# Weights of two modes and strided rows of two batches, each in one transfer

## The chip, the core and the metric

One NeuronCore of a Trainium2 chip runs the whole program. The metric is device time in microseconds (us), of which a run gives one value. A profile is one execution, taken by the hardware profiler; its span (first to last instruction) is mostly some 1.8 us shorter than the device time of the same run (438.82 us of time and 436.9 of span). PE is the matmul engine, DVE the vector engine, ACT the scalar engine, POOL is GpSimd, which here does little but issue transfers (315 of its 339 instructions in the profile of before).

## The reference

Attention of 8 batches, 8 heads, 576 positions, 64 columns per head: heads 0 to 3 see a window of 32 positions ("local"), heads 4 to 7 every 32nd position ("strided"). Its output `x` (8 x 576 x 512) goes through a spectral mix:

```
X = rfft(x, axis=1)[:, :64]                 # 64 modes
Yr = X.real @ w_r[m] - X.imag @ w_i[m]      # per mode m, w_r and w_i: 64 x 512 x 512
Yi = X.real @ w_i[m] + X.imag @ w_r[m]
u = x + irfft(Y)
out = u + relu(u @ w_ch)
```

w_r and w_i are 134 of the 163 MB that the kernel reads. They are float32 in HBM; the transfers turn them into float16 on their way to SBUF (163.22 MB read from HBM in the profile of before, 81.29 MB in the packets of GpSimd's queue, which brings all but the constants).

## The kernel before

GpSimd issues all loads of rows and weights. The modes are passed twice, first for the half of the columns that the strided heads make, then for the other half; numbers from 0 to 127 count the modes of both passes, so that 64 + 51 is mode 51 of the second pass. Each mode has a tile of 4 KB per partition, w_r in partitions 0 to 63, w_i in 64 to 127, and two transfers of 256 KB:

```python
GUEST = {3: ("Y0", 0), 4: ("Y0", 1), 5: ("X0", 0), 6: ("X0", 1)}
GUEST |= {15: ("YT", 0), 16: ("YT", 1)}     # six modes live in tiles that are needed later
...
def w_fetch(n=1):
    for _ in range(n):
        ...
        wt = pw.tile([128, 4, DM], F16, tag="w", name="wt")      # NWBUF = 11 buffers
        for ri, src in enumerate([moe_w_r, moe_w_i] if m else [moe_w_r]):
            nc.gpsimd.dma_start(
                wt[ds(64 * ri, 64)],
                src[m, ds(256 * half, 256), :].rearrange("(p c) e -> p c e", c=4),
            )
```

A mode is 16 matmuls (4 x 4, each 128x128 by 16 columns), after which the next tile is fetched. In the second pass other work lies between the modes: pieces that transpose the attention's output and multiply it by w_ch, about 1.1 per mode, and two per mode in the last ten (`LATE`) before the output stage:

```python
LATE = 10
first = len(work) - 2 * LATE
for m in range(NM - 3):
    mode(1, m)
    if m < NM - 3 - LATE:
        upto = -(-first * (m + 1) // (NM - 3 - LATE))
    else:
        upto = first + 2 * (m - (NM - 4 - LATE))
    for w in work[n:upto]:
        w()
    ...
    if m >= 16 and m % 16 in (4, 8):
        spec(m // 16 - 1, 0 if m % 16 == 4 else 1)
```

Then comes the output stage: 36 blocks of rows, each an inverse transform on PE, a relu on ACT (`rl`), an add on DVE (`osb`), and the store. w_ch, rl and osb took their buffers from the weights' pool.

The softmax here doesn't subtract the row's maximum and nothing guards it: scores larger than these inputs give would overflow.

Of the kernel before, what the change touches and what calls it, by code (L numbers as in the profile page):

```python
# [10 lines left out]
FP = mybir.dt.float32  # L11
F16 = mybir.dt.float16
# [6 lines left out]
DM = 512  # L19
NM = 64  # L20
# [3 lines left out]
JG = [(0, 6), (6, 11), (11, 16)]  # L24
SCALE = float(1.0 / np.sqrt(D))
NEG = -30000.0
NWBUF = 11


def _host_consts():  # L30
# [49 lines left out]
def kernel(  # L80
# [10 lines left out]
    nc = tc.nc  # L91
# [3 lines left out]
    big = ctx.enter_context(tc.tile_pool(name="big", bufs=1))  # L95
# [5 lines left out]
    def psum_pools(**bufs):  # L101
        pctx.close()
        for n, c in bufs.items():
            pss[n] = pctx.enter_context(
                tc.tile_pool(name="ps_" + n, bufs=c, space=PSUM)
            )

    def psum(kind, half=False):
        if half:
            return pss[kind].tile([128, 1024], F16, tag=kind, name=kind)  # L110
        return pss[kind].tile([128, 512], FP, tag=kind, name=kind)
# [16 lines left out]
    def const_load(eng, *which):  # L128
        for n in which:
            eng.dma_start(cs[n][:, 0 : hosts[names.index(n)].shape[1]], drams[n])  # L130
# [13 lines left out]
    def spectra_tile(n):  # L144
        if n == "X0":
            Xh[0] = big.tile([128, 4, B, 2, NM], F16, tag=n, name=n)
        else:
            YS[n] = big.tile([128, 4, 4, 16, 16], F16, tag=n, name=n)

    xb = [px.tile([128, 11, 256], F16, tag="xb", name="xb") for _ in range(B)]  # L150

    pw = ctx.enter_context(tc.tile_pool(name="pw", bufs=NWBUF))
    actx = ctx.enter_context(ExitStack())
# [3 lines left out]
    ring = pat.tile([128, 12, 2048], F16, name="ring")  # L157
# [8 lines left out]



    GUEST = {3: ("Y0", 0), 4: ("Y0", 1), 5: ("X0", 0), 6: ("X0", 1)}
    GUEST |= {15: ("YT", 0), 16: ("YT", 1)}  # L170
    guests = {}
    w_tiles = []
    w_chs = {}

    def w_fetch(n=1):
        for _ in range(n):
            i = len(w_tiles)
            if i >= 2 * NM:
                return
            half, m = 1 - i // NM, i % NM  # L180
            if i in GUEST:
                n, j = GUEST[i]
                if j == 0:
                    guests[n] = big.tile([128, 2, 4, DM], F16, tag=n, name="wt")
                wt = guests[n][:, j]
            else:
                wt = pw.tile([128, 4, DM], F16, tag="w", name="wt")

            for ri, src in enumerate([moe_w_r, moe_w_i] if m else [moe_w_r]):
                nc.gpsimd.dma_start(  # L190
                    wt[ds(64 * ri, 64)],
                    src[m, ds(256 * half, 256), :].rearrange("(p c) e -> p c e", c=4),
                )
            w_tiles.append(wt)

    def w_ch_fetch():
        w_ch = pw.tile([128, 4, DM], F16, tag="w", name="w_ch")
        nc.gpsimd.dma_start(w_ch, moe_w_ch.rearrange("(c p) e -> p c e", p=128))
        w_chs["n"] = w_ch

# [3 lines left out]
    SRC = {2: v, 0: q, 1: k}  # L204
    SLOT = {2: 0, 0: 1, 1: 2}

    def str_in(b, vi):
        return ring[0:72, 3 * (b % 4) + SLOT[vi], :]
# [2 lines left out]
        t = ring[:, ds(2 * (b % 6), 2), :].rearrange("p n x -> p (n x)")  # L211
        return t[:, ds(1152 * vi, 1152)]

    def load_str(b):
        for vi in (2, 0, 1):
            nc.gpsimd.dma_start(
                str_in(b, vi)[0:64],
                SRC[vi][b, 4:8].rearrange("h (c r) d -> (h c) (r d)", r=32)[0:64],
            )
            if b % 2 == 0:  # L220
                n = 3 * (b % 4) + SLOT[vi]
                nc.gpsimd.dma_start(
                    ring[64:72, n : n + 4 : 3, :],
                    SRC[vi][b : b + 2, 4:8].rearrange(
                        "b h (c r) d -> (h c) b (r d)", r=32
                    )[64:72],
                )

    def load_loc(*bs):
        for b in bs:  # L230
            if b >= B:
                return
            for vi in (2, 0, 1):
                nc.gpsimd.dma_start(
                    loc_in(b, vi),
                    SRC[vi][b, 0:4].rearrange("h (cb i) d -> (h cb) (i d)", i=18),
                )
# [294 lines left out]
    def mode(slot, m):  # L532
        half = 1 - slot
        mi, mg = m % 8, m // 8
        if mi == 0:
            ypt[slot] = psum("y")
        yp = ypt[slot]
        yv = yp.rearrange("p (m e x) -> p m e x", m=8, e=4)
        wt = w_tiles[slot * NM + m]
        pr = ds(0, 128 if m else 64)  # L540
        for e in range(4):
            for c in range(4):
                nc.tensor.matmul(  # L543
                    yv[:, mi, e, :],
                    wt[pr, XC[c], ds(128 * e, 128)],
                    Xh[half][pr, c, :, :, m],
                    start=(c == 0),
                    stop=(c == 3),
                )
        if slot or m not in GUEST:  # L550
            w_fetch()
        ends = {7: 8}
        if slot and mg == 7:
            ends = {5: 6, 7: 2}
        if mi in ends:
            n = ends[mi]
            m0 = mi + 1 - n
            part = (
                slice(None),
                slice(None),  # L560
                mg // 2,
                slice(None),
                ds(8 * (mg % 2) + m0, n),
            )
            src = yp.rearrange("p (m e x) -> p e x m", m=8, e=4)[:, :, :, ds(m0, n)]
            if slot == 0:
                if m == 7:
                    spectra_tile("Y0")
                nc.scalar.activation(out=YS["Y0"][part], in_=src, func=ACTF.Copy)
            else:  # L570
                nc.vector.tensor_tensor(
                    out=YS["YT"][part], in0=src, in1=YS["Y0"][part], op=AluOp.add
                )
# [117 lines left out]


    psum_pools(tp=3, sc=3, av=2)
    load_str(0)
    const_load(nc.scalar, "cI", "cM6", "cM5", "cFs")
    load_str(1)
    const_load(nc.sync, "cMl", "cFl", "cA")
    load_str(2)
    w_fetch(2)

    def str_front(b):
        return [
            lambda: str_v(b, 0), lambda: str_v(b, 1),
            lambda: str_v(b, 2), lambda: str_q(b, 0),
            lambda: str_back(b, 0),
            lambda: str_back(b, 1), lambda: str_q(b, 1),
            lambda: str_k(b, 0),
            lambda: str_k(b, 1), lambda: str_k(b, 2),
        ]

    def loc_front(b):
        if b >= B:
            return [lambda: None] * 8
        return [
            lambda: loc_turn(b, 0, 0), lambda: loc_turn(b, 0, 1),
            lambda: loc_turn(b, 1, 0), lambda: loc_turn(b, 1, 1),
            lambda: loc_turn(b, 2, 0), lambda: loc_turn(b, 2, 1),
            lambda: loc_back(b, 0), lambda: loc_back(b, 1),
        ]
# [19 lines left out]
                )  # L739
    SPLIT = [0, 2, 4, 5, 7, 8, 10]  # L740
    for b in range(B):
        if b < 5:
            load_str(b + 3)
        load_loc(*[(), (), (), (), (0,), (1, 2), (3,), (4, 5)][b])
        w_fetch([3, 3, 2, 2, 2, 1, 1, 1][b])
        front = str_front(b + 1) if b + 1 < B else loc_front(0)
        for t in range(6):
            str_scores(b, t)
            if b > 0:
                if t < 2:  # L750
                    str_values(b - 1, 4 + t)
                elif t == 2:
                    dft(b - 1, 1)
            if t >= 2:
                str_values(b, t - 2)
            for w in front[SPLIT[t] : SPLIT[t + 1]]:
                w()
        if b == 1:
            nc.vector.memset(PL[:, 0:PS0], 0.0)
# [10 lines left out]
    for b in range(B):  # L770
# [12 lines left out]
        n = 0  # L783
        nm = NMODES[b]
        for mi in range(nm):
# [3 lines left out]
            n = upto  # L789
# [5 lines left out]
    ptr = ctx.enter_context(tc.tile_pool(name="ptr", bufs=1))  # L795
# [37 lines left out]
    n = 0  # L833
# [3 lines left out]
    for m in range(NM - 3):  # L837
# [7 lines left out]
        n = upto  # L845
# [11 lines left out]
    held, vps, ups, rls, osbs = {}, {}, {}, {}, {}  # L857
# [5 lines left out]
    def pool_adds(b, t):  # L863
        if (b, t) in ((0, 1), (B - 1, 3)):
            return False
        return t in (1, 3, 4) or (b, t) in ((2, 2), (4, 2))
# [21 lines left out]
    def v_rows(i):  # L888
        b, t = units[i]
        if i not in vps:  # L890
            v_early(i)
        vp = vps.pop(i)
        rows_of(b, t, vp, zzs, False)
        if t % 2 == 0:
            rls[b, t] = rls[b, t + 1] = pw.tile([128, 2, DM], FP, tag="w", name="rl")
        rl = rls[b, t][:, t % 2, :]
        nc.scalar.activation(out=rl, in_=vp, func=ACTF.Relu)  # L897
        if pool_adds(b, t):
            nc.gpsimd.tensor_tensor(out=rl, in0=rl, in1=x_rows(b, t), op=AluOp.add)  # L899
# [48 lines left out]
    for m in range(NM - 3, NM):  # L948
        mode(1, m)
# [6 lines left out]
    for i in range(len(units)):  # L956
        v_rows(i)
        b, t = units[i]
# [42 lines left out]
```

## Time and profile before

| | before |
|---|---|
| device time, median of 3 runs | 437.79 us (437.7 to 438.99) |
| span of the profiled run | 436.9 us |
| DMA engines at 90% or more | about 6 to 393 us |
| GpSimd transfers (weights, all) | 254, 315 |
| PE waiting for weights, 120 to 366 us | 59.3 us |
| PE waiting for weights, after 366 us | 0.8 us |
| modes 62, 63 of the second pass start | 397.04, 397.51 us |

### The profile page before, as it was taken

To read this page: it belongs to the slowest core of one execution; us is meant where nothing else is said; L and a number is where in the kernel's file an instruction comes from. 1 tells how busy PE (TensorE), PEld (TensorE's weight loads), DVE (VectorE), ACT (ScalarE), POOL (GpSimd) and SP (SyncE) were. 2 spreads that over 40 slices of the span, in tenths; PEclk is the share of its full clock that TensorE was granted. 3 is DMA by queue.
4 is the path that set the end of the run, shared out by engine and by line. 5 is a ranking of instruction groups with operands and counts; after the bars stand their busy time and mean duration, and the time that the engine had idled before them with its cause. 6 is when DMAs were issued, how large, how long until landed. Compare 5 with 4: busy or idle time off the path is not lost.

```text
span 436.9 us, 12328 instructions
## 1 busy us (share of the span) xinstructions
PE 334.7 (77%) x5289; PEld 240.8 (55%) x5289; DVE 216.1 (49%) x466; ACT 188.5 (43%) x353; POOL 186.6 (43%) x339
## 2 busy tenths in 40 slices
PE   1977888789887888978884576777585948988994
PEld 1866776657756665766653344454354535654441
DVE  2887778835425233344311133344335443773895
ACT  1686678635544345435442211124022402442882
POOL 6545453333343344434343443443443444320883
PEclk9998899959968768688755558689778868998998
DMA  8999999999999999999999999999999999991687
GB/s 173 206 213 211 211 212 211 210 211 211 213 210 212 213 207 211 212 212 212 212 210 212 212 212 212 211 213 211 198 213 212 211 212 212 211 202 25 265 324 278
DMA packets 31094, 92.20 MB, mean 211 GB/s; under 512 B 6144, under 2 KB 7168, under 8 KB 31040
## 3 DMA queue, kind: packets, MB, share of 16 engines
q0 software_dynamic: 26800, 81.29, 94.5%
q1 hardware_dynamic: 3440, 9.46, 5.8%
q10 hardware_dynamic: 800, 0.67, 0.6%
q8 instruction: 42, 0.69, 0.6%
q14 instruction: 12, 0.10, 0.1%
HBM read 163.22 MB, written 9.44 MB: 395 GB/s over the span
## 4 chain that ended last, share of the span: by engine, by line
DMA 55%; PE 26%; DVE 10%; issue 4%; ACT 2%; POOL 1%; DVEq 0%; POOLq 0%
DMA wt<-in_moe_w_i_dram 49%; DMA wt<-in_moe_w_r_dram 5%; PE y L543 3%; PE sc L641 3%; DVE kz L288 2%; DVE xb L246 2%; PE u L684 2%; PE v L684 2%; PE sc L510 2%; PE v L886 2%; DMA ring<-in_q_dram 2%; PE tp L320 1%; PE sc L349 1%; PE av L370 1%; PE sc L341 1%
## 5 line engine op out<-in xcount | busy, mean ns | idle before, releaser
L543 PE MATMUL y<-X,wt 128*128 128x16 f16 (+1 forms) x2048 | 82.7, 193 | 62.6 <-DMA wt<-in_moe_w_i_dram 60.1
L190 POOL DMA_DIRECT2D wt<-in_moe_w_r_dram x128 | 65.8, 514 | 117.4 <-DMA wt<-in_moe_w_r_dram 25.9
L543 PEld LDWEIGHTS <-wt 128*128 128x128 f16 (+1 forms) x2048 | 72.2, 103 | 77.1 <-issue 55.4
L190 POOL DMA_DIRECT2D wt<-in_moe_w_i_dram x126 | 64.8, 514 | 69.7 <-DMA wt<-in_moe_w_i_dram 51.7
L650 ACT ACTIVATE v<-sc 128x512 f16<-128x512 f32 x32 | 19.0, 597 | 88.3 <-PE sc L641 88.3
L641 PE MATMUL sc<-w_cp,xT 128*128 128x512 f16 (+1 forms) x160 | 48.2, 428 | 0.5 <-DVE xT L613 0.4
L467 ACT ACTIVATE PL<-sc 128x480 f16<-128x480 f32 (+1 forms) x48 | 27.6, 579 | 45.0 <-PE sc L453 44.7
L651 DVE COPY xo<-tp 128x512 f16<-128x512 f16 x32 | 22.1, 692 | 39.7 <-PE tp L649 39.7
L246 DVE TENSOR_TENSOR xb<-av,rec 90x256 f16<-90x256 f32 (+2 forms) x80 | 36.0, 450 | 2.8
L245 DVE RECIPROCAL rec<-av 90x4 f32<-90x4 f32 (+2 forms) x80 | 14.7, 184 | 43.2 <-PE av L482 32.1
L398 DVE COPY qT<-tp 128x576 f16<-128x576 f16 x16 | 12.0, 758 | 38.5 <-PE tp L391 35.0
L256 ACT ACTIVATE v<-tp 128x640 f16<-128x640 f16 (+1 forms) x24 | 19.4, 808 | 20.4 <-PE tp L425 17.1
L356 ACT ACTIVATE PL<-sc 90x360 f16<-90x360 f32 (+1 forms) x48 | 22.9, 489 | 9.5 <-PE sc L349 8.8
L391 PE MATMUL tp<-cI_s,ring 64*64 64x64 f16 x864 | 25.4, 208 | 1.9 <-DVE kz L398 1.2
L899 POOL TENSOR_TENSOR rl<-rl,xo 128x512 f32<-128x512 f32 x16 | 18.3, 1156 | 19.2 <-ACT rl L897 18.8
L916 DVE TENSOR_TENSOR osb<-u,rl 128x512 f32<-128x512 f32 x36 | 23.6, 688 | 2.6 <-PE u L684 1.3
L391 PEld LDWEIGHTS <-ring 64*64 64x64 f16 x864 | 20.1, 121 | 6.7 <-issue 3.7
L437 PE MATMUL sc<-cMl_s,cI_s 128*128 128x480 f16 (+1 forms) x48 | 22.5, 469 | 1.6 <-ACT X L256 1.6
L281 PE MATMUL tp<-cI_s,ring 72*128 72x72 f16 x256 | 15.0, 207 | 10.7 <-DMA ring<-in_v_dram 8.0
L453 PE MATMUL sc<-qT,kz 128*128 128x160 f16 (+1 forms) x160 | 22.6, 269 | 0.3 <-issue 0.3
L593 DVE COPY xT<-tp 128x512 f16<-128x512 f16 x16 | 11.0, 689 | 22.9 <-PE tp L587 22.8
L897 ACT ACTIVATE rl<-v 128x512 f32<-128x512 f32 x36 | 20.4, 597 | 4.2 <-PE v L684 3.5
(98 smaller groups left out, 648.4 us busy)
## 6 DMA issues: line engine op xcount, KB each, us to landing
wt<-in_moe_w_r_dram POOLq DMA_DIRECT2D x128, 256.0 KB, 9.4
wt<-in_moe_w_i_dram POOLq DMA_DIRECT2D x126, 256.0 KB, 9.6
out_dram<-osb SPq DMA_DIRECT2D x14, 512.0 KB, 2.7
ring<-in_v_dram POOLq DMA_DIRECT2D x8, 288.0 KB, 10.4
ring<-in_q_dram POOLq DMA_DIRECT2D x8, 288.0 KB, 10.6
ring<-in_k_dram POOLq DMA_DIRECT2D x8, 288.0 KB, 10.6
ring<-in_v_dram POOLq DMA_DIRECT2D x8, 256.0 KB, 8.4
ring<-in_q_dram POOLq DMA_DIRECT2D x8, 256.0 KB, 8.4
```

The source lines that it names most:

```text
L190: nc.gpsimd.dma_start(wt[ds(64 * ri, 64)], src[m, ds(256 * half, 256), :].rearrange("(p c) e -> p c e", c=4),)
L246: nc.vector.tensor_tensor(out=dst, in0=val.rearrange("p h (q c) -> p h c q", c=4), in1=rec[0:n, 0:pieces] .to_broadcast((n, pieces, 64)) . ...
L356: nc.scalar.activation(out=PS[0:n, ds(POFF[t], 4 * n)], in_=scp[0:n, 0 : 4 * n], func=ACTF.Exp, scale=SCALE,)
L391: nc.tensor.transpose(tp[ds(64 * hp, 64), ds(64 * i, 64)], qn[ds(64 * hp, 64), ds(64 * (9 * g + i), 64)], idn[ds(64 * hp, 64), ds(64 * hp, ...
L437: nc.tensor.matmul(scp[:, 0 : n * times].rearrange("p (h x) -> p h x", h=times), idn, mask_rows("cMl", n, times), start=True, stop=False,)
L453: nc.tensor.matmul(scp[:, ds(col, n)], kzs[par][:, hp, ds(s0, 128)], qTs[par][:, ds(s0, n)], start=False, stop=(i == len(todo) - 1),)
L467: nc.scalar.activation(out=dst, in_=src, func=ACTF.Exp, scale=SCALE)
L543: nc.tensor.matmul(yv[:, mi, e, :], wt[pr, XC[c], ds(128 * e, 128)], Xh[half][pr, c, :, :, m], start=(c == 0), stop=(c == 3),)
L641: nc.tensor.matmul(vp[pr, :], xT[:, ch, cols], w_chs["cp"][:, ch, :], start=(ch == 0), stop=(ch == 3),)
L651: nc.vector.tensor_copy(out=xo[pr].rearrange("p (h q c) -> p h q c", h=2, c=4), in_=tp[pr, 0:512].rearrange("p (h c q) -> p h q c", h=2, c=4),
L897: nc.scalar.activation(out=rl, in_=vp, func=ACTF.Relu)
L916: nc.vector.tensor_tensor(out=osb[:, t % 2, :], in0=up, in1=rls[b, t][:, t % 2, :], op=AluOp.add)
```

## The change

It sets out to halve the number of weight transfers without moving a byte more. A tile holds two modes, one transfer brings w_r of both, a second one w_i of both. Five buffers of twice the size replace eleven. Rows of two batches come together too. w_ch gets a tile of its own; rl moves to buffers that the transposes have left (`xT`) and two more. The last two pairs are still transferred mode by mode. The core of the diff:

```diff
-NWBUF = 11
+NWBUF = 5
-    GUEST = {3: ("Y0", 0), 4: ("Y0", 1), 5: ("X0", 0), 6: ("X0", 1)}
-    GUEST |= {15: ("YT", 0), 16: ("YT", 1)}
+    GUEST = {1: "Y0", 2: "X0", 7: "YT"}
+    w_ch = big.tile([128, 4, DM], F16, name="w_ch")
...
+                wt = pw.tile([128, 2, 4, DM], F16, tag="w", name="wt")
+            for ri, src in enumerate((moe_w_r, moe_w_i)):
+                dst = wt[ds(64 * ri, 64)]
+                rows = src[m : m + 2, ds(256 * half, 256), :].rearrange(
+                    "m (p c) e -> p m (c e)", c=4
+                )
+                dst = dst.rearrange("p m c e -> p m (c e)")
+                ones = range(2)
+                if ri and not m:
+                    ones = [1]
+                elif i < 2 * NM - 4:
+                    nc.gpsimd.dma_start(dst, rows)
+                    continue
+                for j in ones:
+                    nc.gpsimd.dma_start(dst[:, j], rows[:, j])
...
-        if slot or m not in GUEST:
+        if m % 2 and (slot or m // 2 not in GUEST):
             w_fetch()
...   (load_str: rows 0 to 63 of two batches in one transfer; fetch counts per batch halved)
-            rls[b, t] = rls[b, t + 1] = pw.tile([128, 2, DM], FP, tag="w", name="rl")
+            n = len(rls) // 2 % 2
+            rl = ptr.tile([128, 2, 576], FP, tag="xT" if n else "rl", bufs=2, name="rl")
+            rls[b, t] = rls[b, t + 1] = rl[:, :, 0:DM]
```

More of the change, by code (lines that the diff above doesn't have):

```diff
@@ L165 @@
     v16 = [pat.tile([128, 12, 132], F16, name=f"v16_{i}") for i in range(2)]
-    GUEST = {3: ("Y0", 0), 4: ("Y0", 1), 5: ("X0", 0), 6: ("X0", 1)}
-    GUEST |= {15: ("YT", 0), 16: ("YT", 1)}
-    guests = {}
+    GUEST = {1: "Y0", 2: "X0", 7: "YT"}
     w_tiles = []
     w_chs = {}
+    w_ch = big.tile([128, 4, DM], F16, name="w_ch")
     def w_fetch(n=1):
@@ L180, in w_fetch @@
             half, m = 1 - i // NM, i % NM
-            if i in GUEST:
-                n, j = GUEST[i]
-                if j == 0:
-                    guests[n] = big.tile([128, 2, 4, DM], F16, tag=n, name="wt")
-                wt = guests[n][:, j]
-            else:
-                wt = pw.tile([128, 4, DM], F16, tag="w", name="wt")
-            for ri, src in enumerate([moe_w_r, moe_w_i] if m else [moe_w_r]):
-                nc.gpsimd.dma_start(
-                    wt[ds(64 * ri, 64)],
-                    src[m, ds(256 * half, 256), :].rearrange("(p c) e -> p c e", c=4),
-                )
-            w_tiles.append(wt)
+            if i // 2 in GUEST:
+                wt = big.tile([128, 2, 4, DM], F16, tag=GUEST[i // 2], name="wt")
+            else:
+                wt = pw.tile([128, 2, 4, DM], F16, tag="w", name="wt")
[3 more added lines that the diff above has]
+                    "m (p c) e -> p m (c e)", c=4
+                )
+                dst = dst.rearrange("p m c e -> p m (c e)")
[7 more added lines that the diff above has]
+                    nc.gpsimd.dma_start(dst[:, j], rows[:, j])
+            w_tiles.extend((wt[:, 0], wt[:, 1]))
     def w_ch_fetch():
-        w_ch = pw.tile([128, 4, DM], F16, tag="w", name="w_ch")
         nc.gpsimd.dma_start(w_ch, moe_w_ch.rearrange("(c p) e -> p c e", p=128))
@@ L212, in loc_in, with load_str @@
         return t[:, ds(1152 * vi, 1152)]
-    def load_str(b):
+    def load_str(b, nb):
         for vi in (2, 0, 1):
-            nc.gpsimd.dma_start(
-                str_in(b, vi)[0:64],
-                SRC[vi][b, 4:8].rearrange("h (c r) d -> (h c) (r d)", r=32)[0:64],
-            )
+            n = 3 * (b % 4) + SLOT[vi]
+            two = ring[:, n : n + 4 : 3, :]
+            src = SRC[vi][b - b % 2 : b - b % 2 + 2, 4:8].rearrange(
+                "b h (c r) d -> (h c) b (r d)", r=32
+            )
+            if nb == 2:
+                nc.gpsimd.dma_start(two[0:64], src[0:64])
+            else:
+                nc.gpsimd.dma_start(ring[0:64, n, :], src[0:64, b % 2])
             if b % 2 == 0:
-                n = 3 * (b % 4) + SLOT[vi]
-                nc.gpsimd.dma_start(
-                    ring[64:72, n : n + 4 : 3, :],
-                    SRC[vi][b : b + 2, 4:8].rearrange(
-                        "b h (c r) d -> (h c) b (r d)", r=32
-                    )[64:72],
-                )
+                nc.gpsimd.dma_start(two[64:72], src[64:72])
     def load_loc(*bs):
@@ L693 @@
     psum_pools(tp=3, sc=3, av=2)
-    load_str(0)
+    load_str(0, 1)
     const_load(nc.scalar, "cI", "cM6", "cM5", "cFs")
-    load_str(1)
+    load_str(1, 1)
     const_load(nc.sync, "cMl", "cFl", "cA")
-    load_str(2)
-    w_fetch(2)
+    load_str(2, 2)
+    w_fetch()
     def str_front(b):
@@ L741 @@
     for b in range(B):
-        if b < 5:
-            load_str(b + 3)
+        if b in (1, 3):
+            load_str(b + 3, 2)
         load_loc(*[(), (), (), (), (0,), (1, 2), (3,), (4, 5)][b])
-        w_fetch([3, 3, 2, 2, 2, 1, 1, 1][b])
+        w_fetch([2, 1, 1, 1, 1, 1, 0, 0][b])
         front = str_front(b + 1) if b + 1 < B else loc_front(0)
```

## The prediction

> **What bounds the kernel now.** I read the sliced overview first. Its DMA rows:
>
> ```profile
> DMA  8999999999999999999999999999999999991687
> GB/s 173 206 213 211 211 212 211 210 211 211 213 210 212 213 207 211 212 212 212 212 210 212 212 212 212 211 213 211 198 213 212 211 212 212 211 202 25 265 324 278
> ```
>
> One digit is 10.9 us. From the second to the thirty-sixth slice, some 6 to 393 us, the DMA engines are never below 90% busy and move 211 to 213 GB/s, in the stretch where attention fills PE as in the stretch where PE idles. Weights and rows are float32 in HBM and float16 in SBUF, so 212 written is about 424 GB/s read. The rate is a plateau. Then the table of DMA queues:
>
> ```profile
> DMA packets 31094, 92.20 MB, mean 211 GB/s; under 512 B 6144, under 2 KB 7168, under 8 KB 31040
> q0 software_dynamic: 26800, 81.29, 94.5%
> ```
>
> Queue 0 is everything GpSimd issues; the change touches nothing else. In the raw packet records (start, duration, size) between 200 and 300 us I followed one DMA engine: its 4096-byte packets start 304 to 305 ns apart, and after every four comes a 4-byte packet, with the next data packet 21 ns later. So a 256 KB transfer costs each engine 4 x 304.5 + 21 = 1239 ns, and the 4-byte packets repeat at 1239 ns. The engines run without gaps, and the only part of that period that depends on how bytes are cut into transfers is the 21 ns.
>
> Third, who waits. Of PE between 120 and 366 us, of PE from 366 us to the end, and of GpSimd over the whole run:
>
> ```profile
> PE y L543 <- DMA wt<-in_moe_w_i_dram: 59.3, 60, 3.5
> ...
> PE y L543 <- DMA wt<-in_moe_w_i_dram: 0.8, 1, 0.8
> ...
> POOL wt L190 <- DMA wt<-in_moe_w_i_dram: 59.5, 103, 1.7
> ```
>
> PE loses 59 us to weights before 366 us and 0.8 us after. GpSimd waits for earlier landings because the program keeps eight semaphores for its DMAs: the ninth transfer is issued when the first has landed. Eight in flight is about 9.9 us of queued work, so its 0.5 us per issue is hidden.
>
> Last, the chain of waits near the hand-over, and the end of it:
>
> ```profile
> 357.06 9.63 DMA wt<-in_moe_w_i_dram
> 366.82 0.65 PE y L543 x16
> 367.47 0.86 PE sc L641 x4
> ...
> 395.85 0.49 PE y L543 x16
> 396.43 0.57 DVE YT L571
> 397.04 1.12 PE y L543 x32
> ```
>
> Here the bound changes. The matmuls of mode 51 of the second pass start at 366.82, 0.14 after their weights landed. From there the chain holds only PE, DVE and ACT work: each of the last ten modes carries two pieces of other work, and a mode takes about 2.9 us of PE against 2.48 us of DMA. The last weights land at 396.7, the modes that use them start at 397.0 and 397.5. So the time is: DMA until mode 51 has landed (366.7), then 30 us of compute to the last modes, then about 39 us of output work (PE busy 30.6 of the last 37 us).
>
> [...] By the packets, 16 x 8192 bytes read per 304.5 ns is 430 GB/s[...]. [...] 315 GpSimd transfers x 16 = 5040 of the 6144 small packets. A transfer saved is 16 small packets saved, one per engine. [...] successive 256 KB transfers land 1.24 us apart, since eight overlap. I count only the 21 ns.
>
> **The change part by part.**
>
> *Fewer transfers.* The built program of the changed kernel has 184 GpSimd DMAs instead of 315: weights 132 for 254, strided rows 27 for 36, the rest equal. Bytes are equal, packets of data equal. Saved: 131 x 21 ns = 2.75 us of DMA time in all. Up to mode 51's landing it is 114 weight transfers and 9 of rows: 123 x 21 ns = 2.6 us. GpSimd's issue time halves too, but is worth nothing.
>
> *A weight is ready a pair at a time.* One transfer has w_r of modes 2p and 2p+1, the next w_i of both. Before, mode 2p could start after its own two transfers; now it waits until the pair's second large one, which is when 2p+1 is ready as well. The even mode comes 2 x 1.24 = 2.48 us later against its neighbour. While DMA is the bound this costs nothing: PE does two modes' work, 2 x about 1.7 us, then idles, in a period of 4.96 us. It costs where PE takes over. The pair of modes 50 and 51 lands at 366.7 - 2.6 = 364.1. Now PE starts mode 50 there, and mode 50 with the work behind it took 364.27 to 365.86, 1.6 us before PE ran dry. Mode 51 starts at about 364.25 + 1.6 = 365.85, against 366.82: 1.0 us of the 2.6 is left.
>
> *And the next pairs.* Each later pair must also arrive in time for its even mode:
> - Modes 52, 53: landed 371.6, now about 369.0. PE gets there at 365.85 + 2.88 = 368.75, waits to about 369.15. Before, mode 52 started at 369.70: 0.55 us left.
> - Modes 54, 55: landed 376.6, now 374.0, so start about 374.1 or later. PE alone: 369.15 + 2.94 + 1.85 = 373.95. Before 374.49: 0.4 us left.
> - Modes 56, 57: landed 382.4 (one engine was some 0.85 us late there), now 379.7, or 378.9 without that delay; PE alone gets there at 374.1 + 2.92 + 2.66 = 379.7. Before 380.07: 0.25 to 0.4 us left.
> - Modes 58, 59: land at 384.1, PE needs them at 385.2. The last two pairs are moved mode by mode, and the last landing comes at about 394, further ahead of PE than now.
>
> So of 2.75 us of DMA time, about 0.3 to 0.5 us reaches the end.
>
> *Five pair buffers for eleven single ones.* Before, w_ch sat in one of the eleven during the second pass, which left ten; five pairs are ten as well. A pair is freed only by its odd mode. In the DMA-bound stretch that is about 2.3 us after landing, with four pairs (19.8 us of transfers) still queued: DMA stays fed. The delicate place is the first pass's start: mode 0 runs at 94.4 us, the first pair comes free at 97.1, and mode 16, which was fetched ahead before, now waits for that. But the local rows queued ahead of it keep DMA busy to about 108.7; pair 8 then fills to 113.6, and the next one can be issued at 105.1. No hole, and PE needs pair 8 only at 118.7.
>
> *Strided rows of two batches together.* Batches 4 and 5 are asked for at once, so batch 4's k comes at about 46 us instead of 39.9, against a need at 47 to 48. If it is late by a microsecond, nothing comes of it: PE's weights have 4 to 7 us in hand at modes 17 to 23, and DMA takes over at mode 24.
>
> *Output stage.* rl moves to four buffers of its own, osb has five. A pair of rows takes some 1.75 us; an output tile is held about 5.5 us (two adds, an issue, 2.7 us to landing), an rl about 4.4: 3.1 and 2.5 buffers needed. No gain, no loss. Instruction order on PE, DVE, ACT and SP is the same but for waits.
>
> **Sum.** 437.8 - 0.4 = 437.4 us.
>
> **The rivals.**
> 1. *DMA-bound to the end: the full 2.75 us comes through, 435.0.* For: DMA at 90% and over until 393 us. Against: after 366 us the chain has no DMA, and PE waited only 0.8 us for weights.
> 2. *The pair's latency exceeds the saving, 438.5 to 439.5.* For: 2.48 us against 2.6 us is close, and the packet records show single engines late by 0.5 to 1 us now and then; one that hits pair 26 or 28 of the second pass passes straight to the end. Against: PE had 0.35 to 1.0 us in hand at those modes.
> 3. *Coarse buffers starve DMA, 440 to 447.* For: a hole of x us before 366 us is x us of time, and a pair is freed later than a mode. Against: the sums above leave 5 us and more everywhere. [...]
> 4. *Per-transfer cost is larger than 21 ns, 433 or less.* Against: engines show no other gap.
>
> **Range and chances.** The before runs spread over 1.3 us. Rival 1 gives the lower end and rival 2 the upper: 435.8 to 439.0. Faster than 2% means 429.0, a gain of 8.8 us: over three times the 2.75 us that all saved packets cost[...]. I give it 1%. Slower than 2% means 446.5, only by rival 3: 2%. Within 2%: 97%.
>
> **What would show it right or wrong.** Packets under 512 bytes should fall by 131 x 16 = 2096, to about 4050. The plateau should rise from 211.6 to about 213.4 GB/s, and weights land every 2.46 us per large transfer. Even modes should wait for DMA some 1.5 us or more and odd ones not at all. Mode 51 should start about 1 us earlier, mode 56 about 0.3 us, and the last landing should come near 394 us with PE not waiting for it. A slice under 205 GB/s between 90 and 360 us would mean rival 3. A saving above 1.5 us would mean that PE's work in the last ten modes wasn't what I took it for.

## The result, and the profile after

| | before | after |
|---|---|---|
| device time, median | 438.39 us (437.7 to 439.06, 4 runs) | 436.88 us (436.57 to 437.36, 4 runs) |
| ratio | | 0.9967, interval 0.9944 to 0.999 |
| span of the profiled run | 436.9 | 434.8 |

A ratio is the mean time of one kernel's runs over that of the other's of the same rounds, so not quite the ratio of the medians.

The DMA rows and the queue of the changed kernel:

```profile
DMA  8999999999999999999999999999999999980787
GB/s 174 210 212 213 214 212 213 211 210 212 214 214 212 214 213 214 214 213 214 214 213 213 213 213 214 214 214 213 213 213 214 213 213 215 213 176 13 268 316 287
DMA packets 28995, 92.16 MB, mean 212 GB/s; under 512 B 4048, under 2 KB 5072, under 8 KB 28944
q0 software_dynamic: 24704, 81.28, 94.2%
```

Small packets fell by 2096, from 6144 to 4048, the plateau rose from 211 to 213 GB/s up to 213 to 214, and no slice lies under 210 between 11 and 382 us: no hole. The DMA issues (kind of transfer, count, size, median us from issue to landing):

```profile
wt<-in_moe_w_r_dram POOLq DMA_DIRECT2D x62, 512.0 KB, 18.9
wt<-in_moe_w_i_dram POOLq DMA_DIRECT2D x60, 512.0 KB, 19.4
```

19 us from issue to landing, against 9.4 and 9.6 before, is not a slower transfer; twice as many bytes are queued. At most issues of GpSimd eight transfers are in flight (302 of 315 before, 167 of 184 now), each weight transfer now has 512 KB, and between 200 and 300 us one lands every 2.46 us. PE's longest wait between 120 and 366 us (total us, times, longest):

```profile
PE y L547 <- DMA wt<-in_moe_w_i_dram: 60.7, 37, 4.7
```

60 waits have become 37 longer ones of the same sum: PE now waits once per pair. PE after 365 us, as a timeline (start, us, line, operation, times):

```profile
365.90 0.65 PE L547 MATMUL y<-X,wt 128*128 128x16 f16 x16
...
369.05 0.65 PE L547 MATMUL y<-X,wt 128*128 128x16 f16 x16 [0.20 <-DMA wt<-in_moe_w_i_dram]
...
379.41 0.64 PE L547 MATMUL y<-X,wt 128*128 128x16 f16 x16
...
396.47 1.12 PE L547 MATMUL y<-X,wt 128*128 128x16 f16 x32 [0.72 <-DVE YT L575]
```

These are modes 51, 52, 56 and 62 with 63. Mode 51 starts 0.92 us earlier than before (366.82), mode 62 is 0.57 us earlier (397.04). So of the 2.6 us by which weights land earlier (the pair of mode 51 at 364.1 against 366.7) only 0.57 us are left at the end of the modes.

The span is 2.1 us shorter, though. The missing 1.5 us lie between 397 and 402 us. Busy times by stretch (length, then busy us and count of PE, PEld, DVE, ACT, POOL; granted clock of PE; DMA share; GB/s), first of the kernel before:

```profile
393.70:397.10 3.40, 1.89 (x26) 1.11 (x25) 1.25 (x2) 0.51 (x1) 0.00 (x0) 1.00 0.32 63
397.10:400.50 3.40, 3.40 (x38) 1.70 (x38) 0.29 (x1) 0.00 (x0) 0.00 (x0) 0.51 0.02 5
```

and of the changed kernel:

```profile
392.00:395.40 3.40, 2.61 (x24) 1.44 (x24) 1.39 (x2) 1.04 (x2) 0.00 (x0) 1.00 0.12 23
395.40:398.80 3.40, 2.68 (x50) 1.73 (x47) 0.85 (x2) 0.00 (x0) 0.00 (x0) 1.00 0.00 0
```

PE ran at half clock for 3.4 us in the profile of before, after a stretch in which it was busy for 1.89 of 3.4 us, and not in the other one. Both kernels have the same two short idle spots there (0.79 us for a copy of DVE, 0.72 us for an add). In the clock records of these two profiles every stretch of half or full clock, but for the last one, lasts 3.413 us or a multiple of it; such a step is called a window from here on. Counted in steps of 3.413 us from the last rise of the clock before the place (363.00 us before, 364.66 in the changed kernel), the windows meet at 393.72 and 397.13 us in the one and at 391.96, 395.38 and 398.79 in the other. So the same idle spots can fall into one window or be shared by two. Is the 1.5 us chance, or did the new buffers bring it? That was the first question for experiments; the second was whether the pair's latency is really where 2 of the 2.6 us went.

### The profile page after: what moved, and what is told of

It reads as the page before. It is cut to its first block, busy times and chain, and to the rows that moved or that the text cites. A ratio compares the mean times of both kernels' runs of the same rounds, so it can differ in the third digit from the quotient of the medians.

```text
span 434.8 us, 12063 instructions
## 1 busy us (share of the span) xinstructions
PE 334.7 (77%) x5289; PEld 241.1 (55%) x5289; DVE 215.0 (49%) x466; ACT 188.0 (43%) x353; POOL 129.3 (30%) x208
## 2 busy tenths in 40 slices
DMA packets 28995, 92.16 MB, mean 212 GB/s; under 512 B 4048, under 2 KB 5072, under 8 KB 28944
## 4 chain that ended last, share of the span: by engine, by line
DMA 73%; PE 19%; DVE 2%; issue 2%; ACT 1%; POOL 1%; DVEq 0%; POOLq 0%
DMA wt<-in_moe_w_i_dram 51%; DMA ring<-in_v_dram 7%; DMA ring<-in_k_dram 6%; DMA wt<-in_moe_w_r_dram 4%; DMA ring<-in_q_dram 4%; PE sc L645 3%; PE y L547 3%; PE v L688 2%; PE u L688 2%; PE v L890 2%; PE y L514 1%; PE tp L653 1%; DVE yy L678 1%; PE u L911 1%; DVE xT L597 1%
## 5 line engine op out<-in xcount | busy, mean ns | idle before, releaser
L196 POOL DMA_DIRECT2D wt<-in_moe_w_r_dram x62 | 36.5, 589 | 142.2 <-PE y L547 63.1
L196 POOL DMA_DIRECT2D wt<-in_moe_w_i_dram x60 | 35.4, 590 | 70.6 <-DMA wt<-in_moe_w_i_dram 57.9
L645 PE MATMUL sc<-w_cp,xT 128*128 128x512 f16 (+1 forms) x160 | 51.3, 450 | 0.4 <-DVE xT L617 0.4
L395 PE MATMUL tp<-cI_s,ring 64*64 64x64 f16 x864 | 26.4, 210 | 2.2 <-issue 1.4
L260 ACT ACTIVATE kz<-tp 64x360 f16<-64x360 f16 (+1 forms) x32 | 19.0, 595 | 10.2 <-PE tp L395 8.6
L645 PEld LDWEIGHTS <-xT 128*128 128x128 f16 (+1 forms) x160 | 14.5, 109 | 14.6 <-issue 5.7
```

Source lines behind the costliest of these rows:

```text
L196: nc.gpsimd.dma_start(dst, rows)
L260: nc.scalar.activation(out=out, in_=in_, func=ACTF.Copy)
L395: nc.tensor.transpose(tp[ds(64 * hp, 64), ds(64 * i, 64)], qn[ds(64 * hp, 64), ds(64 * (9 * g + i), 64)], idn[ds(64 * hp, 64), ds(64 * hp, ...
L645: nc.tensor.matmul(vp[pr, :], xT[:, ch, cols], w_chs["cp"][:, ch, :], start=(ch == 0), stop=(ch == 3),)
```

## The experiments

Twelve kernels were run, all with a profile and in three or five rounds; all gave correct results. Their numbers are names only (there is no 8); they are told in the order of the argument.

**1. The changed kernel again.** No edit.

> The changed kernel again, unedited, more rounds and a second profile. The first comparison gave a ratio of 0.9967 with an interval of 0.9944 to 0.999. In its profile the last two modes start 0.57 us earlier than before (396.47 against 397.04), as predicted, but the span is 2.1 us shorter; the other 1.5 us lie between 397 and 402 us, where the profile of before shows PE at half clock for 3.4 us and the changed one does not. Theory A (the clock window is chance and hits both kernels in some runs): a ratio of 0.997 to 0.9985, some runs of each kernel 1.2 to 1.5 us longer than others, and a second profile in which the last modes start near 396.5 again. Theory B (the output stage itself is faster by the new buffers): a ratio of 0.995 to 0.9965 and the output stage 1.5 us shorter in the profile in all runs, without a half-clock window.

437.28 us (436.83 to 438.36, 6 runs), ratio 0.9979 (0.9957 to 1.0002). Mode 62 started at 396.72 in the profile, mode 63 at 397.20, span 435.0, and no half clock after 365 us. The runs: 436.83, 436.87, 436.92, 437.64, 437.98, 438.36, a group and a tail 0.7 us and more above it. Theory A's range for the ratio and the mode was met. But theory B wanted a shorter output stage in every profile of the changed kernel, and it has that too: 38.3 us from mode 62 to the end, as in its first profile, against 39.9 in that of before. Only the kernel before can decide between them.

**5. The kernel before again, as a control.** No edit.

> The kernel before, unedited, as if it were a change: it gives a second profile of it, and the ratio that two equal kernels show. Theory (the half-clock window at 397 us in the first profile of before is chance, since it followed a 3.4 us window in which PE was busy for only 1.9 us): ratio 0.998 to 1.002; if the profiled run is one of the shorter ones (under 438.2 us), no half-clock window between 370 and 430 us and a span of 435 to 435.8 us; if it is one of the longer ones, such a window again. Modes 62 and 63 start between 396.8 and 397.6 unless a window comes before them. Rival (the new buffers of the output stage removed that window): every profile of before shows it and a span near 437.

438.41 us (437.58 to 439.21), ratio to itself 1.0003 (0.9982 to 1.0024). The profiled run was one of the shorter ones (437.76). The same place in it:

```profile
392.40:395.80 3.40, 2.61 (x19) 1.37 (x17) 1.39 (x2) 1.19 (x2) 0.00 (x0) 1.00 0.52 104
395.80:399.20 3.40, 2.68 (x54) 1.85 (x53) 0.85 (x2) 0.00 (x0) 0.00 (x0) 1.00 0.04 8
```

No half clock, the idle spots shared by two windows, mode 62 at 397.31, span 436.0 (0.2 us over the expected range). The old buffers run without the half-clock window, so theory B is out: the window of the first profile was chance. Profile against profile without such a window, the change is worth 436.0 - 435.0 = 1.0 us, 0.6 of it at mode 62 (397.31 to 396.72) and 0.4 after it. The latter is not the blocks of rows, which take the same time, but what follows the last add on DVE, the landing of the last stores and the closing waits. It goes with the kernel and hardly scatters: 4.46 or 4.47 us in four profiles with the changed kernel's transfers (two of that kernel, experiments 4 and 13), 4.79 to 4.93 in three with those of before, 5.44 to 5.55 in three with those of experiment 3; experiments 11 and 2, alone with theirs, have 4.71 and 5.05. Why the transfers of earlier stages matter there is not known.

**2. Pair tiles, but one transfer per mode and part.**

```diff
-                elif i < 2 * NM - 4:
+                elif i < 0:
```

> The changed kernel's pair tiles, but each part of each mode by its own transfer, in the order w_r, w_r, w_i, w_i. 306 GpSimd transfers, so only 9 x 21 ns of DMA time is saved against before. Theory (21 ns per transfer is all that the change saves, and a pair's even mode is ready late): packets under 512 B back near 6000, the mean landing interval per 256 KB back at 1.239 us, mode 51 of the second pass at about 367.1 and mode 56 at about 381 against 380.07 before, so 0.5 to 1 us slower than before, ratio 1.000 to 1.002. Rival (the pair tiles or the buffers bring the gain, not the larger transfers): ratio near 0.997 as with the changed kernel.

439.71 us (437.86 to 440.17), ratio 1.0022 (0.9996 to 1.0047), where the changed kernel had 0.9979 in the same rounds. Mode 51 started at 366.99 and mode 56 at 380.46, against 366.82 and 380.07 before. The packets under 512 B are back at 6000. The direction is the theory's, without the larger transfers the pair tiles win nothing; that they cost something lies within the noise, and mode 62 at 397.37 is only 0.06 to 0.33 us later than in the two profiles of before.

**7. The other direction: each weight transfer of the kernel before in two halves of partitions.**

```diff
-                nc.gpsimd.dma_start(wt[ds(64 * ri, 64)], src[m, ds(256 * half, 256), :]...)
+                for h in range(2):
+                    nc.gpsimd.dma_start(
+                        wt[ds(64 * ri + 32 * h, 32)],
+                        src[m, ds(256 * half + 128 * h, 128), :]...)
```

> The kernel before, but each weight transfer cut in two by partitions: 508 transfers of 128 KB for the weights, same packets of data. Theory (each transfer costs each DMA engine one 4-byte packet and 21 ns, whatever its size): 254 x 21 ns = 5.3 us more DMA, of which the part up to mode 51 of the second pass, 230 x 21 ns = 4.8 us, comes straight through: mode 51 near 371.6, ratio 1.010 to 1.013. The packets under 512 B rise by 254 x 16 = 4064. Rival (a transfer has a fixed cost that overlaps, or eight transfers of 128 KB no longer cover the time from issue to landing): either no loss, or much more than 6 us with idle DMA slices.

470.32 us, ratio 1.0721 (1.0686 to 1.0756): six times the predicted loss. The packets are as the theory wants, 10209 under 512 B, and where the engines are fed, the 4-byte packets of one engine repeat every 630 ns, 2 x 304.5 + 21. But the rival holds for the rest:

```profile
GB/s 177 207 190 182 194 187 208 208 209 212 178 183 192 201 201 193 201 171 195 203 197 179 202 204 182 186 207 204 185 193 202 190 179 208 206 189 105 247 308 257
```

The plateau is broken. Eight transfers of 128 KB are 5.0 us of work (8 x 0.63), and GpSimd's timeline shows what they must cover:

```profile
200.99 0.49 POOL L191 DMA_DIRECT2D wt<-in_moe_w_i_dram  x1
204.57 0.49 POOL L191 DMA_DIRECT2D wt<-in_moe_w_i_dram  x1 [3.09 <-issue]
205.06 0.97 POOL L191 DMA_DIRECT2D wt<-in_moe_w_r_dram  x2
```

GpSimd paused for 3.1 us, waiting for nothing that the profile shows, and the DMA share fell to 0.73 in the 4 us after. It then issues one transfer per 0.49 us at best, against 0.63 us that a transfer lasts, so it catches up slowly. The kernel before has such pauses too, ending at 155.7 and 308.6 (156.1 and 308.7 in its second profile):

```profile
155.74 0.51 POOL L190 DMA_DIRECT2D wt<-in_moe_w_i_dram  x1 [3.40 <-issue]
308.56 0.52 POOL L190 DMA_DIRECT2D wt<-in_moe_w_r_dram  x1 [3.88 <-PE tp L649]
```

The second is put down to PE (to another PE line in the second profile), but it has the same length of 3.9 us there. In all five profiles of kernels with a transfer per mode and part (before, experiments 5 and 12, and 2 and 7) pauses come after the 128th and the 249th transfer that GpSimd issues, whatever the time: 152 and 305 us before, 163 and 316 in experiment 2, 115 and 201 in this one, which pauses again after the 310th, 370th and 491st. In the changed kernel only 2.1 us follow the 128th, no more than other waits of it. The pauses go with the count of transfers and not with the time; why, and what GpSimd does then, is not shown. The kernel before has 9.9 us queued and passes nearly unharmed. So the 21 ns is the whole price of a transfer only while the queue is deep in time. From 315 to 184 transfers it was; from 315 to 569 it was not.

**3. No pairs at the hand-over.** From mode 48 of the second pass on, w_r and w_i of one mode, then of the next.

```diff
+            late = i >= 2 * NM - 16
+            for j, ri in [(j, ri) for j in range(2) for ri in range(2)] if late else [
+                (None, ri) for ri in range(2)]:
...
+                if j is not None:
+                    nc.gpsimd.dma_start(dst[:, j], rows[:, j])
```

> The changed kernel, but from mode 48 of the second pass on each mode's w_r and w_i are transferred singly and one mode after the other, so that an even mode no longer waits for its pair. 12 more transfers, 0.25 us. Theory (the hand-over to PE at mode 51 is where the saving is lost to the pair's latency): mode 51 starts near 364.4 instead of 365.9, modes 62 and 63 near 394.6 to 395, last landing about 394; 1.5 to 2 us faster than the changed kernel, ratio 0.9925 to 0.995 against before. Rival (the saving is lost elsewhere, PE being the bound well before mode 50): no difference from the changed kernel.

437.37 us (435.11 to 438.04), ratio 0.997 (0.9944 to 0.9996): no better than the changed kernel by the clock. In the profile, mode 51 started at 365.10 and mode 58 at 383.92, 1.4 us ahead of the changed kernel run beside it (385.33). Two modes later nothing was left (390.68 against 390.65). The stretches between:

```profile
379.50:382.90 3.40, 3.00 (x43) 2.04 (x40) 2.61 (x6) 1.23 (x3) 1.38 (x3) 1.00 1.07 210
382.90:386.30 3.40, 2.48 (x32) 1.52 (x31) 2.80 (x8) 1.71 (x3) 1.20 (x3) 0.99 1.04 206
386.30:389.70 3.40, 3.40 (x31) 2.06 (x29) 0.69 (x1) 0.97 (x2) 0.00 (x0) 0.50 1.03 205
```

The clock fell to half after a window with PE busy 2.48 of 3.4 us, in which it had waited three times for DVE. (Busy time alone does not decide it, as a window of experiment 4 shows; see the last section.) The profiled run was the longest of the six; the shortest, 435.11, was the shortest run of any kernel up to then. A theory that one can see but not measure needs the disturbance taken away, not more rounds.

**4. Less work in the last modes of the changed kernel.**

```diff
-    LATE = 10
+    LATE = 3
```

> The changed kernel, but only the last three modes before the output stage carry two pieces of other work, not ten; the 14 pieces go to the modes before, where PE waits for weights. Theory (after mode 51 PE is the bound, DMA before): the modes 51 to 60 follow the landings, the last two modes start near 394 instead of 396.5, 2 to 2.6 us faster than the changed kernel, ratio 0.991 to 0.993 against before. Rival (PE has no room before mode 50 either, since its clock is granted at 0.6 to 0.8 there): PE falls behind the landings from mode 10 of the second pass on and nothing is won.

437.65 us, ratio 0.9979 (0.9954 to 1.0004), the same as the changed kernel. I had expected 2 us and more, and that number was wrong on its own terms: the pair of mode 58 lands at 384.5, from mode 58 to mode 62 PE takes 11.4 us (385.60 to 397.04 before), and 384.5 + 11.4 = 395.9, not 394. In the profile mode 58 started at 384.61, mode 62 at 397.45: 12.8 us, with a half-clock window from 386.9 on. And the rival was partly right: with more pieces per mode PE fell behind the landings. Mode 37 started 4.8 us after its pair had landed (335.74 against 331.0), 2.0 us in the changed kernel (331.57 against 329.6), and it was late again at 53.

**9. Keeping PE busy with useless matmuls.** The kernel of experiment 3, with two matmuls after each mode from 40 on.

```diff
+        if m >= 40:
+            keep = psum("av")
+            for _ in range(2):
+                nc.tensor.matmul(keep, idn, v0s[0][:, 2, :], start=True, stop=True)
```

> The changed kernel with single transfers from mode 48 of the second pass on (the kernel that showed mode 58 at 383.9 instead of 385.3 and then lost it in a half-clock window at 386.3), plus two matmuls of no use after each mode from 40 on, so that PE stays busy. Theory (what eats the gain at the hand-over is half-clock windows[...]): the granted clock is full from about 350 us on in the profile, modes 62 and 63 start near 394.7 to 395, ratio 0.991 to 0.995. Rival (PE is the bound there anyway, and the useless matmuls lie on its path): 20 x 2 x 0.22 = 9 us more PE work, of which some comes on top, ratio over 0.998.

438.89 us (438.25 to 439.14), ratio 1.0011 (0.9993 to 1.0029). The granted clock was full from 345.5 us on, as wanted, and the runs lie within 0.9 us of each other. But mode 58 started at 385.47, where experiment 3 had 383.92: PE has no room after mode 51, and each useless pair of matmuls there lies on the path. The rival won. It told where fillers may go: only where PE waits for DVE.

**12, 13 and 10. Fillers only where PE waits for DVE.** In the kernel before, in the changed kernel and in the kernel of experiment 3, run side by side: 14 useless matmuls after mode 50, at four kinds of places where PE stood idle for 0.4 to 0.8 us.

```diff
+    def fill(n):
+        if keep["m"] < 50:
+            return
+        if "t" not in keep:
+            keep["t"] = psum("av")
+        for _ in range(n):
+            nc.tensor.matmul(keep["t"], idn, v0s[0][:, 2, :], start=True, stop=True)
...   fill(1) before each turn of the local half, fill(2) before spec_mm,
...   fill(3) before the output stage's psum pools, again(3) after mode 61
```

> The kernel before with 14 matmuls of no use at the places after mode 50 of the second pass where PE waits for DVE (0.4 to 0.8 us each), so that no 3.4 us window there has PE busy under 2.6 us. A control for the two kernels beside it. Theory (half-clock windows after 363 us make the longer runs of each kernel): no such window in the profile, the runs no longer fall into two groups; median near the shorter group of before, 437.2 to 437.8, ratio 0.997 to 0.999. Rival (windows there matter little or the fillers delay PE): ratio 1.000 or more, runs still spread over 2 us.

> The changed kernel with the same 14 fillers. Theory (without the chance windows the change is worth what mode 62 shows, 0.6 us, and some tenths at the last store): 0.6 to 1.2 us faster than the kernel before with fillers, near 436.3 to 436.8, ratio 0.995 to 0.997. Rival A (all 2.75 us of the DMA saving come through once the clock is full): 2.5 us faster than the kernel before with fillers. Rival B (the gain measured so far was the chance windows alone): equal to the kernel before with fillers.

> The changed kernel with single transfers, mode after mode, from mode 48 of the second pass on, and the same 14 fillers. Theory (the pair's latency at the hand-over takes about 1.4 us, which showed at mode 58 and was lost again in a half-clock window): mode 58 near 383.9, modes 62 and 63 near 395.3 to 395.8, 1.0 to 1.5 us faster than the changed kernel with fillers, ratio 0.992 to 0.994. Rival (the hand-over is not the place): no faster than the changed kernel with fillers.

| kernel | median us | ratio to before | runs |
|---|---|---|---|
| before | 438.61 | | 437.49 to 439.46 |
| before, fillers | 438.10 | 0.9992 (0.9976 to 1.0007) | 437.24 to 438.80 |
| changed, fillers | 437.89 | 0.9986 (0.9972 to 1.0) | 437.35 to 438.37 |
| changed, singles from mode 48, fillers | 436.14 | 0.9946 (0.9931 to 0.9961) | 435.22 to 436.68 |

None of the three profiles has a half-clock window after 366 us. Even so the first kernel missed what was expected of it: 438.10 us and not 437.2 to 437.8, a ratio that may as well be 1, and six runs that still spread over 1.6 us (the eleven of before over 2.0). So it is not shown that half-clock windows after 366 us make the longer runs; the fillers may also cost what they win. The third is 1.75 us faster than the second, and the two differ only in how the last 16 modes are transferred. It is also faster than the kernel before; the changed kernel without fillers was not run beside it (0.9946 against its 0.9967 and 0.9979, with intervals that overlap). Its timeline at mode 51 and modes 62 and 63:

```profile
364.22 0.65 PE L546 MATMUL y<-X,wt 128*128 128x16 f16 x16 [0.39 <-DMA wt<-in_moe_w_i_dram]
...
394.65 1.12 PE L546 MATMUL y<-X,wt 128*128 128x16 f16 x32
```

Mode 51 starts 2.6 us earlier than before, mode 62 2.4 us; against the kernel before with the same fillers (366.43 and 396.80) both are 2.2 us. That is most of the DMA saving. 0.8 us of it is lost again after the last add (5.55 us against 4.79). Mode 62 also came 0.7 us earlier than I expected, probably because the fillers stand where PE used to stand idle and no window was halved (granted clock 1.00 from 366 to 399 us).

The first two kernels differ by 0.2 us only, where I had expected 0.6 to 1.2. The profile of the second shows one reason:

```profile
363.14 0.68 PE L547 MATMUL y<-X,wt 128*128 128x16 f16 x16
...
365.75 0.69 PE L547 MATMUL y<-X,wt 128*128 128x16 f16 x16
...
367.36 0.65 PE L547 MATMUL y<-X,wt 128*128 128x16 f16 x16
```

These are modes 49, 50 and 51. The pair of modes 48 and 49 landed at 360.4 in this run, 0.9 us later than in experiment 1; PE, at half clock until 366 (0.50 from 362 to 366 us), came to mode 50 a microsecond after its weights, and the late start went straight to the end. Whether the other five runs had such a late pair I can't see.

**6. The rl tiles back in the weights' pool.**

```diff
-            n = len(rls) // 2 % 2
-            rl = ptr.tile([128, 2, 576], FP, tag="xT" if n else "rl", bufs=2, name="rl")
-            rls[b, t] = rls[b, t + 1] = rl[:, :, 0:DM]
+            rls[b, t] = rls[b, t + 1] = pw.tile([128, 2, DM], FP, tag="w", name="rl")
```

> The changed kernel, but the output stage's rl tiles come from the weights' pool again, whose five pair buffers they share with the output tiles. By the holding times in the trace (4.4 us for rl, 5.5 us for osb, a pair of rows each 1.75 us) the two need 2.5 + 3.1 = 5.6 buffers. Theory: the output stage becomes 1 to 4 us longer, ratio 1.000 to 1.007 against before; so the move of rl only pays for the coarser pool and is no gain of itself. Rival (the move is worth 1.5 us by itself, which is the excess over the predicted gain): loses just that and no more, about 0.9985 to 1.001; the profile would then show it between 397 and 402 us and not spread over the stage.

442.83 us (441.88 to 444.11), ratio 1.0103 (1.008 to 1.0127). A bit more than the theory's range, and spread over the stage, as it said: from mode 62 (398.51) to the end it is 43.3 us, 5.0 more than in experiment 1. Another 1.8 us of this profile were lost before mode 62, where a half-clock window lies from 387.5 us on. ACT's waits in the output stage:

```profile
ACT rl L901 <- DVE osb L920: 6.9, 8, 1.6
```

ACT waits eight times until an add on DVE has freed a buffer. So the move of rl wins nothing by itself; it pays for five coarse buffers in place of eleven fine ones.

**11. Strided rows one batch at a time.**

```diff
-        if b in (1, 3):
-            load_str(b + 3, 2)
+        if b < 5:
+            load_str(b + 3)
```

> The changed kernel with the strided rows loaded as before, one batch at a time: 9 more transfers. Theory (9 x 21 ns of DMA, 0.2 us, and batches 4 and 6 arrive earlier, which nothing needs because PE has 1 us and more in hand at the modes before DMA becomes the bound): no measurable difference from the changed kernel, ratio 0.996 to 0.999; mode 51's weights land 0.1 to 0.3 us later than 364.1 to 364.5. Rival (the paired rows hold the attention back): the first mode's start moves forward by over 1 us and the kernel is faster than the changed one by as much.

437.50 us (436.43 to 440.22), ratio 0.9986 (0.9961 to 1.0012), the changed kernel within the noise. The first mode started at 93.01 us, within the 91.9 to 97.2 of all kernels; mode 51's weights landed at 364.1, so even the 0.2 us of nine transfers is not seen. This part of the change does nothing that can be measured.

## Why the prediction was right

The measured 436.88 us lies within 435.8 to 439.0 and 0.5 us from 437.4; the repeated kernel gave 437.28.

*Fewer transfers.* Right to the packet: 2096 fewer. Right in time: 2.6 us expected at mode 51's landing, 2.6 and 2.5 measured (366.7 and 367.0 before, 364.1 and 364.5 after). A rival that was not named is that the deeper queue covers GpSimd's two pauses. By the landings of single engines it is not that: a landing shows as 16 semaphore updates, as many as there are DMA engines, at mode 51 of before the last of them 4.04 us after the first, and mode 51 started 0.14 us after the last. From mode 15 to mode 33 of the second pass, across the pause at 308.6, the last engine's gain over the kernel before grew from 1.96 to 2.32 us (1.74 to 2.36 in the second pair of profiles), where 18 transfers saved make 0.38. The first engine to finish, 4 us and more ahead, did run dry there: its gain jumped from 2.8 to 4.6 us. Experiment 7 adds the condition that the step did not name: the queue must stay full, which it took from the before trace as given.

*A pair at a time.* Right. Mode 51 was expected at 365.85 and came at 365.90, mode 52 at 369.15 and came at 369.05, mode 54 at 374.1 or later and came at 374.02 (366.43, 369.44 and 374.41 in the second profile, so a match to 0.1 us is partly luck). The even modes wait, the odd ones don't. Experiment 10 showed the saving without the cost (1.75 us faster than with it); experiment 2, the cost without the saving, points the same way but not clear of noise (1.0022, 0.9996 to 1.0047).

*What is left.* 0.3 to 0.5 us were expected; at mode 62 it is 0.57 and 0.59 in the two pairs of profiles that were compared above, 0.32 and 0.84 if they are paired the other way, and in the pair with fillers the changed kernel is 1.0 us later (397.79 against 396.80, the profile with the late pair). So single profiles agree with the estimate and can't confirm it to a few tenths. The first comparison was larger, 1.5 us by the medians and 2.1 by the spans, and the prediction had called a saving above 1.5 us a sign that it had the last ten modes wrong. They were as expected; by the spans the excess is the half-clock window in the profile of before, and 0.4 us or so after the last add, for which the prediction had no term. Why the medians of the four runs differ as much is not shown. The prediction had no term for the clock either. It took PE's durations after 366 us from one trace, at full clock there (1.00 from 366 to 397 us), and a single run can be off by the 1.1 to 1.5 us that one window cost here.

*Buffers.* Right: no hole between 11 and 382 us. That rl must leave the pool was seen in the sum of buffers (3.1 + 2.5 against five), and experiment 6 confirms it with 5.5 us against the changed kernel of experiment 1, part of it by a half-clock window.

*The rivals.* Rival 1, the full 2.75 us, was false for this kernel, but experiment 10 shows what it takes to make it nearly true. Rival 2 named single late engines; experiment 13's profile is such a case. Rivals 3 and 4 did not occur.

*What stays open.* The exact worth of the change: three comparisons gave ratios of 0.9967, 0.9979 and, with fillers on both sides, 0.9986 against 0.9992. That is between 0.2 and 1.5 us, positive each time, with intervals as wide as that. Nor is it shown how often a half-clock window strikes each kernel; I know it from single profiles only.

## What to carry to other kernels

Here, with the DMA engines at 90% and over, larger transfers saved their small packets and no more, 2.6 us for 123 transfers, and most of that reached the end only when the consumer at the hand-over could start on less than a whole transfer (experiment 10: mode 62 starts 2.4 us earlier than before, and the time is 1.75 us under that of experiment 13). In a case like this one, use large transfers where the consumer waits anyway, small ones for the last stretch before compute becomes the bound. Check how many microseconds are queued, not how many transfers, before cutting transfers smaller: eight in flight were 9.9 us of work in the kernel before and 5.0 us in experiment 7, which took 32 us longer. When two runs of one kernel differ by more than the effect, look into the profile for the disturbance (here the clock explains the spans of two profiles, not the spread of the runs) and build the comparison without it.

## What the runs show of transfers, pauses and the clock

- What a transfer costs with others in flight: with eight in flight 123 transfers fewer brought mode 51's landing forward by 2.6 us, 21 ns each; 9.9 us of queued work were enough, with 5.0 us (experiment 7) some 32 us were lost.
- Pauses of GpSimd between issues: 3.1 to 3.9 us after the 128th and the 249th transfer in five profiles of four kernels.
- Half clock after partly busy windows: after windows with PE busy 1.83 (experiment 4), 1.89 (before) and 2.48 (experiment 3) of 3.4 us the next was at half clock, after 2.61 and 2.68 (the changed kernel) it was not. PE's busy time as the profile has it does not separate the two: windows with 2.44 us (experiment 4, from 380.1) and with 1.83 (the changed kernel, from 262.3) were followed by full clock. So no limit is given here. One half-clock window cost 1.1 to 1.5 us.
- Instruction loads beside the data transfers: queue 8 of the profile of before, of the kind "instruction", is 42 packets of 16 KB, 0.89 to 1.32 us each, with a median of 0.95. Over the run the first and the last engine of a weight transfer drift apart, from 3.0 us at 120 us to 4.0 at 360 us in the kernel before and from 3.1 to 6.4 us in the changed one. That the packets cause the drift was not tested.
